# Products of the last MLP blocks as pairs of 64-column halves of the PE array

## The chip, the cores and the metric

The kernel runs on one core of a Trainium2 chip. A core has a matrix engine (PE, with its weight loads listed apart as PEld), a vector engine (DVE), a scalar engine (ACT), a general engine (POOL), a queue engine for transfers (SP), and 16 DMA engines that all queues share. The metric is the device time of one execution in microseconds. The kernel before took 306.42 us as the median of five runs: 306.84, 306.89, 304.28, 306.42 and 304.47 us.

## The reference

A retention layer without softmax is followed by an MLP:

```
q, k, v: 8 batches x 8 heads x 576 positions x 64, float32
scores = (q @ k^T) / 8,  times gamma_h^(i-j) where i >= j, else 0
attn   = scores @ v                       (per batch and head)
x      = attn as 4608 tokens x 512
h      = x @ w_in                         (512 -> 2048)
g      = h * clip(h + 3, 0, 6) / 6
out    = g @ w_out                        (2048 -> 512), float32
```

## The kernel before

**Retention.** Each batch's 576 positions are four chunks of 128 and a tail of 64; two tails share one chunk, so there are 36 chunks. Queries and keys are scaled with powers of gamma while they are cast to fp16, which leaves a plain causal mask for the scores and a running 64x64 state per head for everything before the chunk. `ret1` computes the scores of a chunk: 8 matmuls in 4 pairs (line 283), each with 64 rows of the array (the head dimension) and 128 columns, two heads side by side in the upper and lower half of the rows. DVE multiplies them with the mask (line 294). `ret2` computes the outputs into a PSUM tile `xp`: for each of 4 head pairs, two matmuls of scores times values (line 308) and two of state times queries (line 314, or 321 for tails). Each has all 128 rows and 64 columns of the array; the two of a pair (`z` = 0 and 1) write the PSUM partitions 0 to 63 and 64 to 127. Eight more of that kind (line 333) update the state.

**MLP.** Tokens are taken in nine blocks of 512: blocks 0 to 7 are the first 512 positions of each batch, block 8 holds the eight tails. All blocks together are worked in the order 0, 1, 2, 3, 4, 5, 6, 8, 7. The first product (`up`, line 377) makes 16 groups of 128 hidden units per block, each group 4 matmuls of 128 rows, 128 columns and 512 moving columns. (Blocks 1 and 2, and a few groups of block 0, use `up_half`, line 393, with 256.) ACT and DVE turn each group into a slice of the fp16 tile `g` (lines 360 and 365). The second product is, for all blocks but 0, a scheme of Strassen's kind: 7 products instead of 8 (`product`, line 491), with 16 matmuls of 128 x 128 x 256 each. Four of the seven use sums of quarters of `g` (tiles `ss`), which DVE builds in `enc` (line 455). The products end in the accumulators A, B, C and D; ACT and DVE move them out (lines 497 to 520), and SP stores them. Block 0 uses the plain form (line 420).

**Order.** The order of all work is written out by hand in the string `PROGRAM` (lines 36 to 78), one word per step: `s25` is `ret1` of chunk 25, `o25` its `ret2`, `u5.9` the hidden group 9 of block 5, `e5.1.0.4` a part of `enc`, `P5.0` to `P5.6` the seven products of block 5 in the order P1, P5, P6, P2, P7, P4, P3; `c` are casts, `l` loads, `x` transposes by DMA. Each engine follows its instructions in this order. The steps `s` and `o` of the later chunks are set between the steps `u` and `P` of the earlier blocks. The last retention step, `o35`, stands before `P6.6`; from there to the end PE has only MLP work: block 8, then block 7.

**PE's three shapes.** So PE meets matmuls of three kinds: all rows and columns (`u`, `P`; called wide below), half the rows (`s`), and half the columns (`o`). In the profile's operand lists they are `128*128`, `64*128` and `128*64`.

**PSUM.** The hidden groups and the accumulators share four PSUM buffers (tag `mm`); `xp`, the scores and the state have their own.

Of the kernel before, what the change touches and what calls it, by code (L numbers as in the profile page):

```python
# [83 lines left out]
def kernel(  # L84
# [9 lines left out]
    nc = tc.nc  # L94
    B, H, S, D = q.shape
    NTOK, DM = out.shape
    DFF = moe_w_in.shape[1]
    P = 128
# [4 lines left out]
    NFC = DFF // P  # L103
    NCC = DM // P
    BLK = 512
    gamma = [1.0 - 2.0 ** (-5.0 - h) for h in range(H)]
    lng = [float(np.log(g)) for g in gamma]

# [14 lines left out]
    win16 = const.tile([P, NCC, DFF], FP16)  # L123
    wout16 = const.tile([P, NFC, DM], FP16)
    tmat = [const.tile([P, NFC // 2, 256], FP16, name=f"tmat{i}") for i in range(4)]
    xtail = const.tile([P, NCC, BLK], FP16)
    ident = const.tile([P, P], FP16)
    zero16 = const.tile([P, BLK], FP16)
    NS16 = 2
# [121 lines left out]
    def warm(ps, n, w=P):  # L251
        for _ in range(n):
            nc.tensor.matmul(ps, zero16[:, 0:P], zero16[:, 0:w], start=True, stop=True)
# [46 lines left out]
    def ret2(c):  # L300
# [24 lines left out]
        if kind == 0:  # L325
            if t == 0:
                state[0] = psum.tile([P, HP, D], FP32, tag="st", name="state")
                xts[b] = work.tile([P, NCC, BLK], FP16, tag="xt", bufs=3,
                                   name="xt")
# [25 lines left out]
    def g_new(kb):  # L355
        gs[kb] = work.tile([P, NFC, BLK], FP16, tag="g", bufs=2, name="g")

    def hswish(ph, dst):
        u = work.tile([P, BLK], FP32, tag="u", bufs=3, name="u")
        nc.scalar.activation(u, ph, ACTF.Relu, bias=0.5,  # L360
                             scale=1.0 / 6.0)
        sh = list(dst.shape)
        uv = u if len(sh) == 2 else u.rearrange("p (a i) -> p a i", a=sh[1])
        pv = ph if len(sh) == 2 else ph.rearrange("p (a i) -> p a i", a=sh[1])
        nc.vector.scalar_tensor_tensor(out=dst, in0=uv, scalar=1.0,  # L365
                                       in1=pv, op0=ALU.min, op1=ALU.mult)

    def up(kb, fc, nwarm=0):
        if kb not in gs:
            g_new(kb)  # L370
        g = gs[kb]
        xt = xts[kb] if kb < B else xtail
        ph = psum.tile([P, BLK], FP32, tag="mm", bufs=4, name="ph")
        if nwarm:
            warm(ph[:, 0:P], nwarm)
        for m in range(NCC):
            nc.tensor.matmul(ph, win16[:, m, P * fc:P * fc + P], xt[:, m, :],  # L377
                             start=(m == 0), stop=(m == NCC - 1))
        hswish(ph, g[:, fc, :])

    def up_half(kb, hb, fcs, nwarm=0):

        if kb not in gs:
            g_new(kb)
        g = gs[kb]
        xt = xts[kb]
        ph = psum.tile([P, BLK], FP32, tag="mm", bufs=4, name="ph")
        cs = slice(256 * hb, 256 * hb + 256)
        if nwarm:
            warm(ph[:, 0:P], nwarm)  # L390
        for j, fc in enumerate(fcs):
            for m in range(NCC):
                nc.tensor.matmul(ph[:, 256 * j:256 * j + 256],  # L393
                                 win16[:, m, P * fc:P * fc + P], xt[:, m, cs],
                                 start=(m == 0 and j == 0), stop=(m == NCC - 1),
                                 skip_group_check=True)
        d = fcs[1] - fcs[0]
        hswish(ph, g[:, fcs[0]:fcs[1] + 1:d, cs])

    def store(kb, i0, osb_ap, n0, nn):  # L400

        if kb < B:
            base = kb * S + i0
            nc.sync.dma_start(out[base:base + P, n0:n0 + nn], osb_ap)
        else:
            for z in range(2):
                base = (i0 // TAIL + z) * S + MAIN
                nc.sync.dma_start(out[base:base + TAIL, n0:n0 + nn],
                                  osb_ap[z * TAIL:(z + 1) * TAIL, :])
# [6 lines left out]
    def down_plain_part(kb, pos, f0, f1):  # L416
        g = gs[kb]
        for fc in range(f0, f1):
            for mc, po in enumerate(pos):
                nc.tensor.matmul(po, g[:, fc, P * mc:P * mc + P],  # L420
                                 wout16[:, fc, :],
                                 start=(fc == 0), stop=(fc == NFC - 1))

    def down_plain_end(kb, pos):
        for mc, po in enumerate(pos):
# [8 lines left out]
    HF = NFC // 2  # L434
# [24 lines left out]
    def wq(i, j):  # L459
        return wout16[:, i * HF:(i + 1) * HF, j * 256:(j + 1) * 256]  # L460

    def product(kb, name):
        g = gs[kb]
        d = dn.setdefault(kb, {})

        def gq(i, j):
            return lambda fc, m: g[:, j * HF + fc,
                                   i * 256 + m * P:i * 256 + m * P + P]

        def sq(w):  # L470
            t_ = ssum[(kb, w)]
            return lambda fc, m: t_[:, fc, m * P:m * P + P]

        acc, first, last, lhs, rhs = {
            "P1": ("A", True, False, gq(0, 0), wq(0, 0)),
            "P2": ("A", False, True, gq(0, 1), wq(1, 0)),
            "P6": ("B", True, False, None, tmat[1]),
            "P7": ("B", False, False, None, tmat[2]),
            "P4": ("D", True, True, gq(1, 1), tmat[3]),
            "P5": ("C", True, False, None, tmat[0]),  # L480
            "P3": ("C", False, True, None, wq(1, 1)),
        }[name]
        if lhs is None:
            lhs = sq({"P6": 2, "P7": 3, "P5": 1, "P3": 4}[name])
        if first:
            d[acc] = psum.tile([P, 2, 256], FP32, tag="mm", bufs=4,
                               name="acc" + acc)
        ps = d[acc]
        for fc in range(HF):
            for m in range(2):  # L490
                nc.tensor.matmul(ps[:, m, :], lhs(fc, m), rhs[:, fc, :],  # L491
                                 start=(first and fc == 0 and m == 0),
                                 stop=(fc == HF - 1 and m == 1),
                                 skip_group_check=True)
        if name == "P1":
            d["X"] = work.tile([P, 2, 256], FP32, tag="X", bufs=1, name="X1")
            nc.scalar.copy(d["X"], ps)
        elif name == "P6":
            d["W"] = work.tile([P, 2, 256], FP32, tag="W", bufs=1, name="W1")
            nc.vector.tensor_tensor(out=d["W"], in0=ps, in1=d["X"], op=ALU.add)  # L500
        elif name == "P5":
            return
        else:
            if name == "P7":
                d["Z"] = work.tile([P, 2, 256], FP32, tag="Z", bufs=1, name="Z1")
                nc.vector.tensor_tensor(out=d["Z"], in0=ps, in1=d["X"],
                                        op=ALU.add)
                ps = d["C"]
            ob = work.tile([P, 2, 256], FP32, tag="osb", bufs=4, name="osb")
            if name == "P2":  # L510
                nc.scalar.copy(ob, ps)  # L511
                i, j = 0, 0
            elif name == "P7":
                nc.vector.tensor_tensor(out=ob, in0=ps, in1=d["Z"], op=ALU.add)
                i, j = 1, 1
            elif name == "P4":
                nc.vector.tensor_tensor(out=ob, in0=ps, in1=d["Z"], op=ALU.add)
                i, j = 1, 0
            else:
                nc.vector.tensor_tensor(out=ob, in0=ps, in1=d["W"], op=ALU.add)  # L520
                i, j = 0, 1
            if kb < B:
                base = kb * S + i * 256
                nc.sync.dma_start(
                    out[base:base + 256, j * 256:(j + 1) * 256]
                    .rearrange("(m p) n -> p m n", p=P), ob)
            else:
                for m in range(2):
                    store(kb, i * 256 + m * P, ob[:, m, :], j * 256, 256)
# [87 lines left out]
    for h in range(H):  # L617
        z = h % 2
# [95 lines left out]
```

## Time and profile before

| | |
|---|---|
| median of five runs | 306.42 us |
| the profiled execution | 306.84 us, its span 304.6 us |
| PE busy | 292.7 us (96%), 2879 matmuls |
| weight loads (PEld) busy | 200.9 us (66%) |
| DVE, ACT, POOL busy | 240.1, 145.7, 102.9 us |
| line 377, 128x512 | mean 379 ns from start to end |
| line 491, 128x256 | 273 ns |
| line 308, 128x128 in half the columns | 230 ns |

The durations of matmuls overlap: the next one starts long before the one before has ended. What a matmul costs is the distance between the starts of two that follow each other, and this is read from the timeline. A timeline row gives the start, the length, the engine, the line, the operation and how many instructions were merged into it; the row's length reaches to the end of the last of them. "Idle before" tells how long the engine had nothing to do before a row, and what ended that.

### The profile page before, as it was taken

The page shows a single profiled execution, that of the slowest core. Times are in us where ns is not written, and L with a number is a line of the kernel's source. Part 1 is how long each engine was busy: PE and PEld are TensorE (multiplying, and loading weights), DVE is VectorE, ACT ScalarE, POOL GpSimd, SP SyncE. Part 2 cuts the span into 40 slices and gives each one's busy share as a digit, 9 for nine tenths or more (in the row PEclk, how much of TensorE's full clock was granted, in tenths as well). Part 3 has the DMA queues.
Part 4 walks back from the last instruction along what each step waited for, and adds up shares of the span by engine and source line. Part 5 has one row for each costly group of instructions (what it writes and reads, how often), then busy time and mean ns, then how long its engine had stood idle before and what let it go on. Part 6 is the DMA issues. An engine that isn't in the chain of part 4 may idle for free.

```text
span 304.6 us, 7130 instructions
## 1 busy us (share of the span) xinstructions
PE 292.7 (96%) x2879; PEld 200.9 (66%) x2879; DVE 240.1 (79%) x341; ACT 145.7 (48%) x267; POOL 102.9 (34%) x116
## 2 busy tenths in 40 slices
PE   8789999898999999999999999999999999999995
PEld 3566444687887888646864686468655874684584
DVE  6656845899976999889778996998699768856963
ACT  2578713865236643466147423763376226405610
POOL 5254554884048635445554141334200000000000
PEclk9879999999999999999999999999999999999999
DMA  6999999999999999999999998997603030014003
GB/s 217 303 322 383 253 310 213 225 209 209 196 156 217 229 212 215 195 205 206 237 214 241 242 237 185 225 265 88 178 3 69 28 114 0 1 43 97 2 0 138
DMA packets 149728, 53.93 MB, mean 177 GB/s; under 512 B 134848, under 2 KB 145088, under 8 KB 149696
## 3 DMA queue, kind: packets, MB, share of 16 engines
q1 hardware_dynamic: 120128, 46.15, 69.6%
q10 hardware_dynamic: 29568, 7.34, 17.4%
q8 instruction: 22, 0.36, 0.5%
q14 instruction: 10, 0.08, 0.1%
HBM read 36.70 MB, written 9.44 MB: 151 GB/s over the span
## 4 chain that ended last, share of the span: by engine, by line
PE 88%; DVE 4%; DMA 3%; ACT 2%; issue 0%; SPq 0%
PE ph L377 31%; PE accB L491 10%; PE ph L393 9%; PE accA L491 9%; PE accC L491 9%; PE accD L491 5%; PE po L420 4%; PE xp L308 4%; PE sc L283 4%; DMA g<-in_k_dram 3%; PE xp L314 2%; DVE g L365 2%; PE state L333 1%; DVE ss L455 1%; ACT wout L220 1%; DVE tmat L580 1%
## 5 line engine op out<-in xcount | busy, mean ns | idle before, releaser
L360 ACT ACTIVATE u<-ph 128x512 f32<-128x512 f32 x144 | 84.6, 597 | 65.3 <-PE ph L377 36.8
L365 DVE SCALAR_TENSOR_TENSOR g<-u,ph 128x512 f16<-128x512 f32 x144 | 94.7, 683 | 25.3 <-ACT u L360 24.2
L377 PE MATMUL ph<-xt,win 128*128 128x512 f16 x368 | 82.1, 379 | 0.0
L377 PEld LDWEIGHTS <-win 128*128 128x128 f16 x432 | 41.4, 98 | 47.7
L491 PEld LDWEIGHTS <-ss 128*128 128x128 f16 x512 | 49.0, 98 | 6.9 <-DVE ss L455 0.9
L176 POOL TENSOR_TENSOR qk<-st,tq 128x512 f16<-128x512 f32 x29 | 30.4, 1048 | 51.4 <-DMA st<-in_q_dram 20.9
L176 POOL TENSOR_TENSOR v<-st,tkv 128x512 f16<-128x512 f32 x29 | 32.1, 1111 | 36.5 <-DMA st<-in_v_dram 13.9
L294 DVE TENSOR_TENSOR at<-sc,mask 128x1024 f16<-128x1024 f32 (+1 forms) x34 | 39.0, 1154 | 5.4 <-PE sc L283 5.3
L491 PEld LDWEIGHTS <-g 128*128 128x128 f16 x384 | 36.9, 98 | 6.1 <-issue 0.8
L393 PE MATMUL ph<-xt,win 128*128 128x256 f16 x288 | 34.1, 277 | 0.4 <-ACT xt L338 0.4
L176 POOL TENSOR_TENSOR qk<-st,tkv 128x512 f16<-128x512 f32 x26 | 29.3, 1126 | 10.7 <-PE accA L491 6.7
L491 PE MATMUL accA<-wout,g 128*128 128x256 f16 x256 | 30.6, 273 | 0.8 <-DVE g L365 0.8
L393 PEld LDWEIGHTS <-win 128*128 128x128 f16 x288 | 27.9, 99 | 4.5 <-issue 0.5
L491 PE MATMUL accB<-tmat,ss 128*128 128x256 f16 x256 | 30.7, 273 | 0.1
L338 ACT ACTIVATE xt<-xp 128x512 f16<-128x512 f32 x32 | 19.1, 598 | 20.2 <-PE xp L314 16.9
L455 DVE TENSOR_TENSOR ss<-g 128x1024 f16<-128x1024 f16 (+1 forms) x30 | 23.9, 807 | 0.3
L308 PE MATMUL xp<-at,v 128*64 128x128 f16 x288 | 20.7, 230 | 1.3 <-ACT xt L338 0.8
L308 PEld LDWEIGHTS <-v 128*64 128x64 f16 x288 | 14.8, 112 | 7.3 <-issue 4.8
L511 ACT COPY osb<-accA 128x512 f32<-128x512 f32 x8 | 4.7, 586 | 28.2 <-PE accA L491 28.2
L344 ACT CAST s<-state 64x256 f16<-64x256 f32 x48 | 17.3, 360 | 0.5
L420 PE MATMUL po<-wout,g 128*128 128x512 f16 x64 | 15.0, 379 | 0.6 <-DVE g L365 0.5
L491 PE MATMUL accC<-wout,ss 128*128 128x256 f16 x128 | 15.3, 273 | 0.0
(88 smaller groups left out, 273.8 us busy)
## 6 DMA issues: line engine op xcount, KB each, us to landing
st<-in_v_dram SPq DMA_DIRECT2D x32, 256.0 KB, 6.0
out_dram<-osb SPq DMA_DIRECT2D x32, 256.0 KB, 4.9
st<-in_q_dram SPq DMA_DIRECT2D x28, 256.0 KB, 5.6
st<-in_k_dram SPq DMA_DIRECT2D x28, 256.0 KB, 6.0
wst<-in_moe_w_in_dram SPq DMA_DIRECT2D x4, 512.0 KB, 7.4
tmat<-in_moe_w_in_dram SPq DMA_DIRECT2D x4, 512.0 KB, 8.8
wst<-in_moe_w_out_dram SPq DMA_DIRECT2D x4, 512.0 KB, 10.3
g<-in_moe_w_out_dram SPq DMA_DIRECT2D x4, 512.0 KB, 6.0
```

The costliest lines, as they stand in the source:

```text
L176: eng.tensor_tensor(out=dst, in0=st[:, ix, :, :], in1=tab.unsqueeze(2).to_broadcast([P, H, D]), op=ALU.mult)
L294: nc.vector.tensor_tensor(out=dst, in0=src, op=ALU.mult, in1=m[:, :].unsqueeze(1).to_broadcast([P, n, P]))
L308: nc.tensor.matmul(xp[rows[z], p, :], vt[:, 2 * p + z, :], at[:, z, p, :], start=(p == 0), stop=False, skip_group_check=True)
L338: nc.scalar.activation(xts[b][:, :, t * P:(t + 1) * P], xp, ACTF.Copy, scale=0.125)
L344: nc.scalar.copy(s16[rows[z], :, rows[z]], sp[rows[z], :, :])
L360: nc.scalar.activation(u, ph, ACTF.Relu, bias=0.5, scale=1.0 / 6.0)
L365: nc.vector.scalar_tensor_tensor(out=dst, in0=uv, scalar=1.0, in1=pv, op0=ALU.min, op1=ALU.mult)
L377: nc.tensor.matmul(ph, win16[:, m, P * fc:P * fc + P], xt[:, m, :], start=(m == 0), stop=(m == NCC - 1))
L393: nc.tensor.matmul(ph[:, 256 * j:256 * j + 256], win16[:, m, P * fc:P * fc + P], xt[:, m, cs], start=(m == 0 and j == 0), stop=(m == NCC - 1),
L420: nc.tensor.matmul(po, g[:, fc, P * mc:P * mc + P], wout16[:, fc, :], start=(fc == 0), stop=(fc == NFC - 1))
L455: nc.vector.tensor_tensor(out=dst, in0=a, in1=c, op=op)
L491: nc.tensor.matmul(ps[:, m, :], lhs(fc, m), rhs[:, fc, :], start=(first and fc == 0 and m == 0), stop=(fc == HF - 1 and m == 1), skip_grou ...
```

## The change

Two tuples name the blocks that get the new form. `mul` issues one wide matmul as before, or two in its place. Of the two, the first loads the columns 0 to 63 of the stationary operand and writes the PSUM partitions 0 to 63; the second takes the columns 64 to 127 and the partitions 64 to 127. Both stream the same moving operand. The first product is issued so in blocks 5, 6, 8 and 7, the second in blocks 4, 5, 6, 8 and 7. Everything else, the order in `PROGRAM` included, stays. (Each matmul in the kernel's text becomes a weight load and a matmul on PE.)

```diff
     BLK = 512
+    COL_UP, COL_DOWN = (5, 6, 8, 7), (4, 5, 6, 8, 7)
...
+    def mul(ps, lhs, rhs, start, stop, halves=True):
+
+        if not halves:
+            nc.tensor.matmul(ps, lhs, rhs, start=start, stop=stop,
+                             skip_group_check=True)
+            return
+        for z in range(2):
+            nc.tensor.matmul(ps[z * D:z * D + D], lhs[:, z * D:z * D + D], rhs,
+                             start=start, stop=stop, skip_group_check=True)
+
...
         for m in range(NCC):
-            nc.tensor.matmul(ph, win16[:, m, P * fc:P * fc + P], xt[:, m, :],
-                             start=(m == 0), stop=(m == NCC - 1))
+            mul(ph, win16[:, m, P * fc:P * fc + P], xt[:, m, :],
+                m == 0, m == NCC - 1, kb in COL_UP)
         hswish(ph, g[:, fc, :])
...
             for mc, po in enumerate(pos):
-                nc.tensor.matmul(po, g[:, fc, P * mc:P * mc + P],
-                                 wout16[:, fc, :],
-                                 start=(fc == 0), stop=(fc == NFC - 1))
+                mul(po, g[:, fc, P * mc:P * mc + P], wout16[:, fc, :],
+                    fc == 0, fc == NFC - 1, kb in COL_DOWN)
...
         for fc in range(HF):
             for m in range(2):
-                nc.tensor.matmul(ps[:, m, :], lhs(fc, m), rhs[:, fc, :],
-                                 start=(first and fc == 0 and m == 0),
-                                 stop=(fc == HF - 1 and m == 1),
-                                 skip_group_check=True)
+                mul(ps[:, m, :], lhs(fc, m), rhs[:, fc, :],
+                    first and fc == 0 and m == 0, fc == HF - 1 and m == 1,
+                    kb in COL_DOWN)
```

`up_half` is changed in the same way; it is used by blocks 0 to 2 alone, which are in neither tuple.

More of the change, by code (lines that the diff above doesn't have):

```diff
@@ L392, in up_half @@
             for m in range(NCC):
-                nc.tensor.matmul(ph[:, 256 * j:256 * j + 256],
-                                 win16[:, m, P * fc:P * fc + P], xt[:, m, cs],
-                                 start=(m == 0 and j == 0), stop=(m == NCC - 1),
-                                 skip_group_check=True)
+                mul(ph[:, 256 * j:256 * j + 256],
+                    win16[:, m, P * fc:P * fc + P], xt[:, m, cs],
+                    m == 0 and j == 0, m == NCC - 1, kb in COL_UP)
         d = fcs[1] - fcs[0]
@@ L490, in product @@
             for m in range(2):
-                nc.tensor.matmul(ps[:, m, :], lhs(fc, m), rhs[:, fc, :],
-                                 start=(first and fc == 0 and m == 0),
-                                 stop=(fc == HF - 1 and m == 1),
-                                 skip_group_check=True)
+                mul(ps[:, m, :], lhs(fc, m), rhs[:, fc, :],
+                    first and fc == 0 and m == 0, fc == HF - 1 and m == 1,
+                    kb in COL_DOWN)
         if name == "P1":
```

## The prediction

> **What bounds the kernel now.** I began with the page's busy rows, to see which engine is full, and where.
>
> ```profile
> PE 292.7 (96%) x2879; PEld 200.9 (66%) x2879; DVE 240.1 (79%) x341; ACT 145.7 (48%) x267; POOL 102.9 (34%) x116
> PE   8789999898999999999999999999999999999995
> DVE  6656845899976999889778996998699768856963
> PEclk9879999999999999999999999999999999999999
> ```
>
> PE is full from about the tenth slice on, at full clock. That alone doesn't say that PE sets the pace, since a busy PE can still be running below its rate. So the second view is the table by stretches, cut where the change bites: the first product in the new form is P4.0, which I place at 171.6 us (the accA rows of the trace; block 4's first product is the seventh of them), and the last retention step ends at 246.7.
>
> ```profile
> core 0: us, PE busy (x) PEld busy (x) DVE busy (x) ACT busy (x) POOL busy (x), PEclk, DMA share, GB/s
> 171.60:247.00 75.40, 75.40 (x817) 52.76 (x812) 66.50 (x90) 33.66 (x65) 16.43 (x15) 1.00 0.72 142
> 247.00:301.00 54.00, 53.88 (x368) 35.50 (x365) 38.31 (x55) 21.88 (x37) 0.00 (x0) 1.00 0.16 46
> 301.00:304.60 3.60, 0.00 (x0) 0.00 (x0) 0.61 (x1) 0.00 (x0) 0.00 (x0) 0.81 0.37 127
> ```
>
> For 129 us PE is never idle but for 0.12 us; after it come one DVE addition and the last store, 3.6 us. The list of waits of PE in this stretch is empty. So what shortens PE's own sequence there shortens the kernel, if nothing else then becomes late. The third view, the timeline of PE, shows at what rate it works and where it loses time:
>
> ```profile
> 201.94 1.91 PE L491 MATMUL accA<-wout,g 128*128 128x256 f16 x16
> 203.69 1.91 PE L491 MATMUL accC<-tmat,ss 128*128 128x256 f16 x16
> 205.53 0.40 PE L283 MATMUL sc<-qkT 64*128 64x128 f16 x8
> 205.86 0.25 PE L308 MATMUL xp<-at,v 128*64 128x128 f16 x2
> 205.94 0.22 PE L314 MATMUL xp<-qkT,s 128*64 128x128 f16 x2
> ...
> 206.33 0.29 PE L333 MATMUL state<-v,qk 128*64 128x64 f16 x8
> 206.55 1.92 PE L491 MATMUL accB<-tmat,ss 128*128 128x256 f16 x16
> 208.31 1.91 PE L491 MATMUL accA<-wout,g 128*128 128x256 f16 x16
> 210.15 0.25 PE L308 MATMUL xp<-at,v 128*64 128x128 f16 x2
> 210.23 0.22 PE L314 MATMUL xp<-qkT,s 128*64 128x128 f16 x2
> ```
>
> *Rate of wide matmuls.* From 201.94 to 203.69 are 16 of them: 109 ns each. In the chain, 40 of line 377 take 8.63 us, 216 ns each. The two give 0.416 ns a moving column and 2.6 ns besides.
>
> *Rate of pairs.* From 205.94 to 206.33 are seven column pairs of 128: 55.7 ns a pair. The line above gives 128 x 0.416 + 2.6 = 55.8. So the two halves run at once, and a pair costs what one wide matmul of that length would. Starts of single instructions show the second half 3 to 4 ns behind the first, and the next pair 52 to 53 ns later.
>
> *Changes of shape.* The last accC matmul starts at 203.69 + 1.91 - 0.273 = 205.33; the scores follow at 205.53, 0.20 us later where 0.109 is the rate. In the same way every change of shape shows a gap. From single starts, which repeat within 2 ns from 130 us to 247, the excess at the change and at the next step is:
>
> ```
> wide -> half rows     96 + 10 = 106 ns
> half rows -> columns  90 + 24 = 114
> columns -> wide       99 + 10 = 109
> wide -> columns       94 + 24 = 118
> columns -> half rows  99 + 11 = 110
> half rows -> wide     92 + 11 = 103
> ```
>
> Nothing else exceeds the rate in this stretch, but two waits of some 65 ns for an `ss` tile, at 265.9 and 292.0.
>
> **The change part by part.**
>
> *Changes of shape removed.* Going through PROGRAM from P4.0 on, 25 boundaries are touched. Columns to wide, now without any change: o23 P4.0, o24 P4.3, o25 P4.6, o26 u5.2, o27 u5.6, o28 P5.2, o31 u6.3, o32 u6.12, o33 P6.0, o34 P6.4, o35 P6.6: 11 x 109 ns = 1.20 us. Wide to columns, likewise: P5.3 o29, u6.1 o30, P6.5 o35: 3 x 118 = 0.35 us. Still a change, but of another kind: before s25 to s29 and s32 to s35 (9 times) columns instead of wide to half rows, 9 x 4 = 0.04 us dearer; after s30 and s31 half rows to columns instead of wide, 114 instead of 103 at most, 0.02 us dearer. Block 4's first product stays wide, so nothing changes before P4.0. Saved: 1.55 - 0.06 = **1.5 us**, all of it on PE and before 246.7.
>
> *Pairs for wide matmuls.* First product: 4 blocks x 16 x 4 = 256 pairs of 512. Second: 5 x 7 x 16 = 560 pairs of 256. 816 pairs in all, so PE shows 2879 + 816 = 3695 matmuls. No row shows a pair of 256 or 512. The nearest is the pair of 128, and it lies on the line of the wide ones, so I take 0 ns a pair. Bounds: above, the 3.3 ns between the halves might come on top of each pair, 816 x 3.3 = +2.7 us; below, the 2.6 ns that every start costs might vanish, -2.1 us, but the pair of 128 pays it too, so a gain has no row for it.
>
> *Weight loads.* [...] The rows:
>
> ```profile
> L491 PEld LDWEIGHTS <-ss 128*128 128x128 f16 x512 | 49.0, 98 | 6.9 <-DVE ss L455 0.9
> L308 PEld LDWEIGHTS <-v 128*64 128x64 f16 x288 | 14.8, 112 | 7.3 <-issue 4.8 <-DVE osb L514 0.2
> ```
>
> A half's load takes 112 ns where a whole one takes 98. If the two loads of a pair went one after the other, a pair of 256 would take 224 ns instead of 109, and the 560 of them 64 us more. But in retention four instructions (two such loads, two matmuls) fit into each 56 ns, and the state's pairs of 64 columns come every 30 ns; the loads of the two halves run side by side and behind the matmuls before. A pair of 256 leaves them 109 ns. [...]
>
> [...]
>
> *Instruction supply.* PE gets 1632 instructions more. The page's queue 8 fetched 22 packets of 0.36 MB in all, 16 KB each; one took 0.9 to 1.4 us, about one for every 256 of PE's instructions. After the change some 28. In the new products 256 instructions last 7 us; the trace before has 261 in 7 us at 114 us, with DMA at its fullest and no gap on PE beyond the changes of shape. Cost 0; if each of the some 15 fetches after 171 us stood open, 15 x 1.2 = 18 us.
>
> *Who is late next.* ACT and DVE get no work and no wait. A PE that is 1.5 us ahead by 247 asks them to be quicker by as much over 75 us, of which DVE is busy 66.5. In its tightest 20 us (190 to 210: 19.34 busy) three changes go, 0.33 us of PE's time, against 0.66 idle. Single margins: a PSUM buffer for a hidden group comes free 0.4 us (u6.14) to 2 us before PE wants it; the `ss` tile of P5.2 and that of P6.2 are there 0.6 us before, and one change of shape (0.11) goes between the last `u` and them; transposed chunks land 2.7 us or more before their scores. None is used up. What lies behind 247 us, the two 65 ns waits included, moves forward as a whole.
>
> *Sum.* 306.84 - 1.5 = 305.3 us for an execution like the profiled one. That one lies 0.4 us above the median, so 306.42 - 1.5 = **304.9 us**, 0.5% less. The runs shown lie at 304.3 to 304.5 and 306.4 to 306.9, with nothing between, so a median can fall 2 us to either side without the kernel being another. About 1% is what a measurement of this kernel can tell from no change.
>
> **The rivals.**
>
> *The pair is dearer than one wide matmul (slower).* Place: every pair, the 129 us after 171.6. The change loses from 1.5 us / 816 = 1.8 ns a pair, and loses over 1% from 5.6 ns. With the offset between the halves on top, 304.9 + 2.7 = 307.6; with the slower load on the path (14 ns), 304.9 + 11.4 = 316.3. For it: no row at 256 or 512, two streams of one operand instead of one for long times, and the load's row. Against it: the 55.7 ns. Chance 0.13, 0.06 of it at the small price.
>
> *Instructions come too late.* 304.9 + 18 = 323. For it: the rate is above the one shown over spans longer than 7 us (448 in 12.2 us; before at most 431 in 14 us). Against it: fetches are short beside 7 us. Chance 0.03.
>
> *The gain is waited off.* DVE, 97% busy from 190 to 210, holds PE back, and the time stays at 306.4. For it: u6.14's 0.4 us. Against it: DVE's own gaps there end with ACT, which waited for PE. Chance 0.11.
>
> *The change does more than counted*, by over 1%: 303 or less. No row for it; 0.04.
>
> **How the numbers follow.** The forecast keeps 0.69. About an eighth of it falls below 303.4, by the spread of the runs. Faster by over 1%: 0.09 + 0.04 = 0.13. Slower by over 1%: 0.07 + 0.03 = 0.10. Within 1%: 0.77. The range goes from 302.7 (the forecast with a median 2 us low) to 307.6 (the small price of a pair); it leaves out the dear cases above and a few per cent below.
>
> **What the profile would show.** Right: rows of line 491 and 377 with `128*64`, pairs of 256 every 109 ns and of 512 every 216; no gap between `o` and `u` or `P` from 171.6 on; P6.0 about 1.2 us earlier than 234.4, the first group of block 8 starting at about 247.0 instead of 248.5; 52.4 us from there to the end of PE, as before; 3695 matmuls. Wrong: over 111 ns a pair, gaps every 256 instructions, or waits of PE for DVE between 190 and 247.

## The result, and the profile after

The changed kernel takes 305.35 us (median; 302.69 to 307.48), the kernel before 305.88 us in the same comparison. The ratio is 0.9972, with a 95% interval of 0.9956 to 0.9988: 0.28% faster, or 0.86 us, with 0.37 to 1.35 us in the interval. The plain medians lie 0.53 us apart, the means 0.80 (standard error 0.24). Forecast was 1.5 us. So the direction and the range held, and 0.6 us of the gain is missing. That the median comes within 0.5 us of the forecast's 304.9 is in part luck: the forecast started from 306.42, the median of five runs, and over more runs the kernel before lies 0.54 lower. The profiled execution took 305.91 us, its span is 303.7.

First the page of the kernel after: busy rows, the queue that fetches instructions, and the weight loads of the halves from `ss`.

```profile
PE 289.3 (95%) x3695; PEld 208.9 (69%) x3695; DVE 238.8 (79%) x341; ACT 145.2 (48%) x267; POOL 103.5 (34%) x116
...
q8 instruction: 29, 0.48, 0.7%
...
L366 PEld LDWEIGHTS <-ss 128*64 128x64 f16 x640 | 34.5, 110 | 0.5 <-DVE ss L464 0.3
```

The matmuls are 3695, as counted. The instruction queue fetched 29 packets (before 22; 28 were forecast). A half's weight load takes 110 ns on average, where a whole one took 98, so the slower load is really there. PE's busy time fell all the same, by 3.4 us, but that also holds differences of the first 125 us, where executions of one kernel differ (two of before by 2.7 us).

The table by stretches shows whether PE is still the bound; the cuts are moved to this execution.

```profile
core 0: us, PE busy (x) PEld busy (x) DVE busy (x) ACT busy (x) POOL busy (x), PEclk, DMA share, GB/s
171.20:245.50 74.30, 74.30 (x1275) 58.09 (x1276) 66.39 (x91) 33.73 (x65) 15.36 (x15) 1.00 0.84 145
245.50:300.10 54.60, 54.47 (x760) 40.73 (x754) 39.02 (x56) 22.07 (x37) 0.00 (x0) 1.00 0.16 46
```

PE is busy throughout at full clock, and weight loads rose to 58.09 us beside it without showing as a gap. PE's list of waits is empty from 165 us on. The timeline of PE has the same steps as the one shown of before:

```profile
201.94 1.91 PE L366 MATMUL accA<-wout,g 128*64 128x256 f16 x32
203.69 1.91 PE L366 MATMUL accC<-tmat,ss 128*64 128x256 f16 x32
205.54 0.40 PE L284 MATMUL sc<-qkT 64*128 64x128 f16 x8
...
206.34 0.29 PE L334 MATMUL state<-v,qk 128*64 128x64 f16 x8
206.46 1.92 PE L366 MATMUL accB<-tmat,ss 128*64 128x256 f16 x32
208.21 1.91 PE L366 MATMUL accA<-wout,g 128*64 128x256 f16 x32
209.96 0.22 PE L309 MATMUL xp<-at,v 128*64 128x128 f16 x2
```

Three things are read here. A product of 32 halves takes 1.75 us from start to start (201.94 to 203.69), as 16 wide ones did: a pair costs 109 ns. From the state's first matmul to accB's is 0.12 us (206.34 to 206.46), where it was 0.22: the change from columns to wide is gone. From accA to the next outputs is 1.75 us, where it was 1.84: wide to columns is gone as well. The scores still cost a change on both sides: from accC to them are 1.85 us and from them to the outputs 0.32, where it was 1.84 and 0.33.

To leave out what lies ahead of the change, I measure from the first scores of chunk 24 to the end of PE's last matmul. First before, then after:

```profile
170.69 0.40 PE L283 MATMUL sc<-qkT 64*128 64x128 f16 x8
...
298.97 1.91 PE L491 MATMUL accC<-wout,ss 128*128 128x256 f16 x16
```

```profile
171.21 0.40 PE L284 MATMUL sc<-qkT 64*128 64x128 f16 x8
...
298.06 1.91 PE L366 MATMUL accC<-wout,ss 128*64 128x256 f16 x32
```

PE ends at 300.88 and 299.97. That is 130.19 us before and 128.76 after: **1.43 us less**, against 1.5 forecast. So the two profiles show nearly the full gain, and the comparison of all runs 0.86 us. The experiments ask what each term of the sum is worth, and where the rest stays.

### The profile page after: what moved, and what is told of

Its sections match the earlier page's. It is cut to its first block, busy times and chain, and to the rows that moved or that the text cites. A ratio compares the mean times of both kernels' runs of the same rounds, so it can differ in the third digit from the quotient of the medians.

```text
span 303.7 us, 8762 instructions
## 1 busy us (share of the span) xinstructions
PE 289.3 (95%) x3695; PEld 208.9 (69%) x3695; DVE 238.8 (79%) x341; ACT 145.2 (48%) x267; POOL 103.5 (34%) x116
## 4 chain that ended last, share of the span: by engine, by line
PE 82%; SPq 5%; DVE 5%; DMA 3%; ACT 1%; POOL 1%; issue 1%; ACTq 0%; POOLq 0%
PE ph L366 18%; PE ph L362 17%; PE accB L366 6%; PE accC L366 6%; PE accA L366 6%; PE po L362 4%; SPq L555 4%; PE accB L362 4%; PE xp L309 3%; DMA tmat<-in_moe_w_in_dram 3%; PE sc L284 3%; PE accA L362 3%; PE accC L362 3%; PE accD L366 3%; DVE g L376 2%; PE accD L362 2%
## 5 line engine op out<-in xcount | busy, mean ns | idle before, releaser
L362 PE MATMUL ph<-xt,win 128*128 128x256 f16 (+1 forms) x464 | 72.6, 313 | 1.9 <-ACT xt L339 1.3
L362 PEld LDWEIGHTS <-win 128*128 128x128 f16 x464 | 44.4, 98 | 25.3 <-issue 2.5
L366 PEld LDWEIGHTS <-win 128*64 128x64 f16 x512 | 28.7, 110 | 24.4
L366 PE MATMUL ph<-xt,win 128*64 128x512 f16 x384 | 42.8, 379 | 0.0
L366 PEld LDWEIGHTS <-ss 128*64 128x64 f16 x640 | 34.5, 110 | 0.5 <-DVE ss L464 0.3
L362 PEld LDWEIGHTS <-g 128*128 128x128 f16 x208 | 19.6, 98 | 11.3 <-issue 2.8
L366 PEld LDWEIGHTS <-g 128*64 128x64 f16 x480 | 26.1, 110 | 0.6
L362 PEld LDWEIGHTS <-ss 128*128 128x128 f16 x192 | 18.4, 98 | 2.7 <-DVE ss L464 0.4
L366 PE MATMUL accB<-tmat,ss 128*64 128x256 f16 x320 | 19.2, 273 | 0.0
L366 PE MATMUL accA<-wout,g 128*64 128x256 f16 x320 | 19.1, 273 | 0.0
```

Source lines behind the costliest of these rows:

```text
L362: nc.tensor.matmul(ps, lhs, rhs, start=start, stop=stop, skip_group_check=True)
L366: nc.tensor.matmul(ps[z * D:z * D + D], lhs[:, z * D:z * D + D], rhs, start=start, stop=stop, skip_group_check=True)
```

## The experiments

Theory 1 is the prediction's: pairs are free, only changes of shape count, and nothing else becomes late. The rivals are dearer pairs, late instructions, and a gain that is waited off.

**Before and after, again.** Neither is edited.

> The kernel before, unchanged, against itself: it shows how far a comparison of this length lies from 1 by chance. Every theory says 306 us and a ratio of 1.000; a ratio beyond 0.998 to 1.002 would mean that the 0.28% measured for the change is within what chance gives.

> The change as it is. Theory 1 (14 changes of shape fewer, pairs cost nothing, all of it comes through): from the scores of chunk 24 to the end of PE 129.4 us where the kernel before takes 130.9, and a ratio of 0.995. Theory 2 (the gain in that stretch is real, but the stretch before it gets slower by some 0.5 us, by instruction supply or placement): the same 129.4, but the scores of chunk 24 start 0.5 us later than in the kernel before, ratio 0.997. Theory 3 (a part of the gain is waited off in some executions): more than 129.8 us in that stretch.

Before gave 306.05 us, ratio 0.9992 (0.9966 to 1.0018). After gave 305.33, ratio 0.9979 (0.9952 to 1.0006), so this comparison alone can't tell it from before. In the new profiles the stretch from chunk 24's scores to PE's end is 130.20 us and 128.76 us. The stretch thus repeats within 0.01 us, and the change is worth 1.44 us in it. (The totals in the expectation, 130.9 and 129.4, are 0.7 us too large on both sides; the difference is what counts.) In these profiles all that varies lies ahead: chunk 24's scores start at 170.69 and 167.99 us in the two profiles of before, at 171.21 and 169.15 in the two of after. In both pairs the change comes later here, by 0.52 and 1.16 us, as the second theory of the expectation has it. But three more profiles, of the next three kernels below, have the code of before up to this place and start at 168.53, 168.71 and 169.21. With a scatter of nearly 3 us from one code, a loss of some 0.5 us ahead of the change can be neither shown nor excluded.

**Pairs in blocks 8 and 7 alone.** Behind the last retention step there is no shape to be matched, so this gives the price of the pair alone.

```diff
-    COL_UP, COL_DOWN = (5, 6, 8, 7), (4, 5, 6, 8, 7)
+    COL_UP, COL_DOWN = (8, 7), (8, 7)
```

> Pairs in blocks 8 and 7 alone: 128 pairs of 512 and 224 of 256, with no retention beside them, so no change of shape goes and one comes (before the first group of block 8). Theory 'a pair costs one wide matmul': from the first group of block 8 to the last product the same 52.4 us within 0.1, the whole +0.1 us. Theory 'the offset between the halves adds up': 352 x 3.3 ns = +1.2 us. Theory 'the slower load is on the path': 352 x 14 ns = +4.9 us.

306.39 us, ratio 1.0001 (0.9972 to 1.003). In the chain of before, `P6.6` and the last product start at

```profile
246.79 1.85 PE accC L491 x16
...
299.13 1.76 PE accC L491 x16
```

which is 52.34 us apart; in the chain of this kernel

```profile
244.64 1.85 PE accC L362 x16
...
297.14 1.77 PE accC L366 x32
```

they lie 52.50 apart. One change, wide to columns, is new between the two (118 ns by the prediction's list; from block 8's own first start to PE's end, as the expectation counts, it is 52.47 us against 52.40); 0.04 us is left for 352 pairs, 0.1 ns a pair. "The pair is dearer" would need 1.8 ns a pair to undo the gain. That rival falls.

**Quarters.** Four parts of 32 columns double the instructions once more, and with them any offset between the parts (3 to 4 ns between halves).

```diff
-        for z in range(2):
-            nc.tensor.matmul(ps[z * D:z * D + D], lhs[:, z * D:z * D + D], rhs,
-                             start=start, stop=stop, skip_group_check=True)
+        for z in range(4):
+            nc.tensor.matmul(ps[z * 32:z * 32 + 32], lhs[:, z * 32:z * 32 + 32],
+                             rhs, start=start, stop=stop, skip_group_check=True)
```

The tuples are again `(8, 7), (8, 7)`.

> Blocks 8 and 7 alone, each wide matmul as four of 32 columns in place of two of 64: PE gets 2112 instructions more than before, 8 in each 109 ns of the second products, 256 of them in 3.5 us. Theory 'only the moving columns count': 52.1 us from the first group of block 8 to the last product, as before, and a time within 0.2 us of before. Theory 'each further part adds its 3 ns': 352 x 9 ns = +3.2 us in that stretch. Theory 'instructions come too late': gaps on PE some every 3.5 us. Beside this: if a longer PE program by itself makes the first 125 us slower (the change came out some 0.7 us short of what its late stretch gained, for 1632 instructions more), the whole is about 0.9 us slower than the stretch explains; if not, the two agree.

306.21 us, ratio 1.0013 (0.9989 to 1.0037). The chain:

```profile
244.82 1.85 PE accC L362 x16
...
286.74 1.75 PE accA L366 x64
...
297.32 1.78 PE accC L366 x64
```

Again 52.50 us, and 64 quarters take 1.75 us, as 32 halves and 16 wholes do. Eight instructions (four loads, four matmuls) every 109 ns leave no gap. "Instructions come too late" falls, and so does an offset that adds up by the part. The expectation asked one thing more: whether a longer PE program slows the first 125 us by itself, which would show as some 0.9 us beyond the stretch. This kernel is 0.4 us slower than before (-0.3 to 1.1 by its interval), and the stretch explains 0.16 us of it; so no such loss shows, but the interval doesn't exclude it.

**Shapes in turn.** In blocks 8 and 7 the hidden groups 0 to 7 are pairs and 8 to 15 wide; `PROGRAM` takes one of each in turn.

```diff
-    COL_UP, COL_DOWN = (5, 6, 8, 7), (4, 5, 6, 8, 7)
+    COL_UP, COL_DOWN = (8, 7), ()
...
-                m == 0, m == NCC - 1, kb in COL_UP)
+                m == 0, m == NCC - 1, kb in COL_UP and fc < 8)
```

> First products of blocks 8 and 7 alone: groups 0 to 7 in halves, groups 8 to 15 wide, second products wide. The order takes them in turn (0, 8, 1, 9, ...), so 16 changes of shape are added per block, 32 in all, and 64 matmuls become pairs. Price of a change as read in the prediction (109 ns columns to wide; 94 ns and up to 24 for wide to columns): 32 x 0.103 to 0.114 = +3.3 to +3.6 us, ratio 1.011 to 1.012. Theory 'a change of shape costs little by itself and the gaps before were those of retention's waits': under +1 us.

309.97 us, ratio 1.0126 (1.0087 to 1.0166). The timeline shows the price at each group:

```profile
247.10 1.05 PE L366 MATMUL ph<-xtail,win 128*64 128x512 f16 x8
248.09 1.04 PE L362 MATMUL ph<-xtail,win 128*128 128x512 f16 x4
249.06 1.05 PE L366 MATMUL ph<-xtail,win 128*64 128x512 f16 x8
```

Groups start 0.97 to 0.99 us apart where 4 x 0.216 = 0.864 is the rate. The chain:

```profile
245.32 1.85 PE accC L362 x16
...
301.29 1.76 PE accC L362 x16
```

`P6.6` and the last product are 55.97 us apart, 3.63 more than before. That is 32 changes at 113 ns; the prediction's 109 and 118 in equal parts would be 113.5.

**All blocks.** If shapes are all that counts, pairs in every block should gain more.

```diff
-    COL_UP, COL_DOWN = (5, 6, 8, 7), (4, 5, 6, 8, 7)
+    COL_UP, COL_DOWN = tuple(range(9)), tuple(range(9))
```

> Pairs in all nine blocks: 75 changes of shape in place of 110 before and 96 with the change. By the prices of the prediction 3.7 us of PE's time less than before, 2.2 less than with the change. Theory 1: what lies after 125 us (0.6 us more than with the change) comes through whole; what lies before it only where PE doesn't wait for loads there; so 302.5 to 304.3, ratio 0.988 to 0.994. Theory 'instructions come too late where the DMA engines are full' : gaps on PE in the first 170 us and no gain, or a loss, over the change.

316.5 us, ratio 1.0301 (1.0259 to 1.0344): a clear miss. (The built program has 79 changes of shape, not the 75 of the expectation.) From chunk 24's scores on it takes 128.76 us, as with the change; the whole loss lies ahead of them. The waits of PE between 90 and 170 us, as engine, line, what it waited for, sum in us, how often, the longest; first before:

```profile
PE xp L308 <- DVE at L294: 0.5, 1, 0.5
PE ph L393 <- ACT xt L338: 0.4, 1, 0.4
```

then with pairs in all blocks:

```profile
PE ph L366 <- DVE g L376: 6.7, 3, 5.2
PE sc L284 <- DMA qkT<-qk: 1.8, 2, 0.9
...
```

PE waits for DVE to finish a hidden group, once for 5.2 us. So something holds back the evacuation of the groups. Two more kernels look for it, one that widens the change by a single block, and one that puts pairs where they hurt and nowhere else.

```diff
-    COL_UP, COL_DOWN = (5, 6, 8, 7), (4, 5, 6, 8, 7)
+    COL_UP, COL_DOWN = (3, 4, 5, 6, 8, 7), (3, 4, 5, 6, 8, 7)
```

> Pairs in block 3 and in the first product of block 4 too: six changes of shape fewer than with the change (90 against 96), 0.6 us of PE's time, all after 122 us. Theory 'PE is the bound from 125 us on and the feed has room': 129.2 us from the scores of chunk 24 to the end of PE as with the change or less, from the first group of block 3 to those scores 44.8 instead of 45.3 us, ratio 0.993 to 0.995. Theory 'the feed of chunks by loads and transposes has no room before 170 us' (what the run with all blocks suggests): waits of PE for scores or for PSUM between 125 and 170 us, and no gain over the change.

```diff
-    COL_UP, COL_DOWN = (5, 6, 8, 7), (4, 5, 6, 8, 7)
+    COL_UP, COL_DOWN = (0, 1, 2), (0, 1, 2)
```

> Pairs in blocks 0 to 2 alone: 13 changes of shape fewer, 1.4 us of PE's time, all before 125 us, where PE also waits for loads. Theory 'PE gets ahead of the feed there, ACT then stands behind transposes whose data aren't loaded, and PSUM isn't freed': PE waits for g of 1 us and more between 105 and 145 us and a time of 309 us or more, as with all blocks. Theory 'the loss with all blocks came from block 3': the time is 306 or less.

From block 3 on: 309.43 us, ratio 1.0084 (1.0057 to 1.0112). Six changes of shape fewer than after, and yet slower; PE waits, but nearly all of it just before 193 us, and only 0.25 us between 125 and 170, where one side had expected it. From chunk 24's scores on its profile takes 133.07 us, 4.31 more than with the change; the medians differ by 4.1. Blocks 0 to 2: 317.82, ratio 1.0388 (1.0348 to 1.0428). The timeline of the first of the two, some rows around the wait (SPq and ACTq are the transfers' issues on SP and ACT):

```profile
184.88 1.60 SPq L162 DMA_DIRECT2D st<-in_v_dram  x2
...
185.77 0.60 ACT L371 ACTIVATE u<-ph 128x512 f32<-128x512 f32 x1 [0.27 <-PE ph L366]
...
190.11 1.28 ACTq L185 DMA_TRANSPOSE qkT<-qk  x1
...
191.50 1.08 ACT L371 ACTIVATE u<-ph 128x512 f32<-128x512 f32 x2 [5.12 <-POOL v L177]
...
192.12 1.28 DVE L376 SCALAR_TENSOR_TENSOR g<-u,ph 128x512 f16<-128x512 f32 x2 [5.04 <-ACT u L371]
...
192.87 0.41 PE L366 MATMUL ph<-xt,win 128*64 128x512 f16 x2 [2.88 <-DVE g L376]
```

ACT stands idle for 5.12 us behind one instruction, the transpose of chunk 28's queries and keys (a step `x`), though two finished groups (`u5.1` and `u5.9`) lie in PSUM. When it goes, ACT, DVE and PE follow within 3 us. The releaser named, a cast on POOL, belongs to chunk 30 (`c30` stands behind `o26` in `PROGRAM`) and gives chunk 28 nothing. What the transpose waited for is seen in the landings: the value load issued at 184.88 us landed at 190.01, and the transpose was issued at 190.11.

The kernel's text is built into lists of instructions for each engine, with their waits; these built programs tell why a transpose should wait for a load. DMAs issued by SP and ACT share eight completion semaphores: in the traces of before and after 208 transfers, 26 on each. The builder hands these out in turn, as it seems in the order in which it places the transfers (the first 40 issued take them in turn), and in the programs each transfer waits until the one before it on its semaphore has landed. In these two traces none is issued earlier; the shortest distance is 0.02 us. In the kernel from block 3 on, the load of 184.88 us and the transpose of 190.11 us have the same one. Chunk 28's transpose, in the built program of before and of after:

```
before: qkT_3104<-qk16_2856  waits DMAHW3_49, DMAHW5_49, DVE_49, Pool_49
after:  qkT_3224<-qk16_2856  waits DMAHW3_49, DMAHW7_49, DVE_49, Pool_49
```

(The number in a semaphore's name, `DMAHW5` or `DMAHW7`, tells which of the eight it is.) The instructions of ACT, DVE, POOL and SP are the same ones, but a transpose shares its semaphore with another load, and that can be one issued later (chunk 29's follows a load issued 5.2 us ahead of it in after, 8.1 us in before). In the kernel with pairs in blocks 0 to 2, the transpose that ends the long wait went at 137.20 us, 0.06 us after the landing (137.14) of a key load issued at 131.42 on the same semaphore. Six transposes in a row (chunks 15 to 20) went 0.06 to 0.10 us after the landing of the transfer before them on their semaphore: three loads, two stores and one transpose. In before these six distances are 2 to 9 us. (Before is not free of such waits: there chunk 22's transpose goes 0.10 us after chunk 21's has landed.) Against before, the transposes' waits differ from chunk 8 on in this kernel and in the one with all blocks, from chunk 22 on with block 3, from chunk 28 on in the change itself, and nowhere in the three kernels that alter blocks 8 and 7 alone. Why pairs move the builder's order was not shown.

A second cost shows in the same kernel (pairs in blocks 0 to 2): PE's row after its wait, and the table cut at the wait. The table's columns are those above, the clock third from the end.

```profile
140.31 5.62 PE L362 MATMUL ph<-xt,win 128*128 128x512 f16 x16 [5.09 <-DVE g L376]
```

```profile
136.00:140.30 4.30, 0.00 (x0) 0.00 (x0) 0.73 (x2) 1.36 (x3) 1.32 (x2) 0.68 1.22 282
140.30:144.30 4.00, 3.99 (x10) 1.43 (x10) 3.04 (x5) 1.69 (x4) 0.00 (x0) 0.50 1.35 194
144.30:148.00 3.70, 3.70 (x46) 1.89 (x44) 3.29 (x5) 2.05 (x5) 1.24 (x2) 0.99 1.38 218
```

After the wait of 5 us PE runs at a clock of 0.50 for some 4 us: ten matmuls in 4.0 us, 427 ns apart instead of 216. That adds some 1.9 us to the 5 us. All of PE's waits between 90 and 170 us sum to 10.1 us in this kernel (0.9 in before); with the 1.9 us this is most of the loss of 12 us.

**Is it a faster PE instead?** It might be that PE merely runs ahead of ACT and DVE. So pairs stay in blocks 0 to 2, but the first and the last matmul of each stretch of MLP work between two retention steps are wide. The changes of shape come back and more: the built program has 152, before has 110.

```diff
+    edge = [False, 0, 0]
...
-        if not halves:
+        edge[1] += 1
+        if not halves or edge[1] == 1 or (edge[0] and edge[1] == edge[2]):
```

(A dozen lines in the loop over `PROGRAM` set `edge`; the tuples are `(0, 1, 2)`.)

> Pairs in blocks 0 to 2 as in the run that lost 12 us, but the first and the last matmul of every stretch of MLP work between two retention steps stay wide. So no change of shape goes and about two come per stretch: PE has some 3.5 us more to do before 125 us than in the kernel before, and isn't ahead of its input. Theory 'the loss comes from waits that the built program got: a transpose shares its completion semaphore with a load issued shortly before, and ACT stands until that load has landed': those waits are nearly the same as in the run that lost, so 314 us or more, with PE waiting over 4 us for g at about 140 us. Theory 'PE got ahead of its input by the changes saved': 306 to 310 us, no such wait.

314.22 us, ratio 1.0254 (1.0208 to 1.0301). PE's waits between 90 and 170 us:

```profile
PE xp L309 <- ACT xt L339: 1.8, 1, 1.8
PE sc L284 <- DMA qkT<-qk: 1.3, 1, 1.3
PE ph L364 <- DVE g L378: 1.3, 1, 1.3
...
```

PE now has more to do than in before, 42 changes or some 4.6 us, which is about half of the loss of 8.4 us. And it still waits, if less: 4.6 us in this stretch, where it was 10.1 with pairs throughout and 0.9 in before. Six transposes (chunks 15 to 20) again go 0.06 to 0.15 us after the landing of the transfer before them on their semaphore. So a PE that runs ahead by the changes saved isn't the cause. The long wait at 140 us, which I had expected to stay above 4 us, did not stay: the longest in this stretch is 1.8 us. And some of this kernel's waits differ from those of the kernel it was made from (five of its 28 transposes have another semaphore), so it doesn't isolate one wait.

**Transposes on SP.** If ACT no longer issues them, a late transpose can't hold up ACT.

```diff
-        nc.scalar.dma_start_transpose(
+        nc.sync.dma_start_transpose(
```

> All matmuls wide as before, but the 28 transposes of the chunks are issued by SP, in the place that they have among the loads in the written order, and not by ACT. All transfers then stand on one queue, and which two share a semaphore no longer hangs on anything but that order. It is the partner of the run with pairs in all blocks and the same issue by SP. Level unknown: SP waits for casts before it can issue later loads; 304 to 325 us.

> Pairs in all nine blocks, transposes issued by SP. Waits of SP, ACT and, but for four, of POOL and DVE are those of its partner with wide matmuls. Theory 'shared semaphores made the loss of 10 us with all blocks, the pairs themselves cost nothing also with the DMA engines full': faster than the partner by 1 to 3.7 us (35 changes of shape fewer). Theory 'pairs in the first blocks run PE ahead of its input or are short of instructions': slower than the partner by several us, as it was on ACT's queue.

Before with this edit takes 320.44 us, ratio 1.046 (1.0422 to 1.0498); all blocks in pairs with it 322.33, ratio 1.052 (1.0478 to 1.0563). The expected gain of pairs in the second over the first didn't come: it is 0.6% slower (four runs of each). PE's waits between 60 and 200 us, in the first and in the second:

```profile
PE sc L283 <- DMA qkT<-qk: 12.5, 4, 5.8
...
```

```profile
PE sc L284 <- DMA qkT<-qk: 15.7, 4, 6.8
...
```

On SP the transposes stand among the loads, and PE waits for transposed chunks in both, for 12.5 and 15.7 us. The edit brings a larger wait of its own, and the pair of runs says nothing for or against the semaphores.

**Pairs only where no wait changes.** Pairs are set by place instead of block: only in the stretches of MLP work between two retention steps from `u5.2` on. In this form every wait of ACT, SP, POOL and DVE in the built program is that of before, and 11 changes of shape go.

```diff
-    COL_UP, COL_DOWN = (5, 6, 8, 7), (4, 5, 6, 8, 7)
+    PAIRED, gap = (26, 27, 28, 29, 30, 31, 32, 33, 34, 35), [-1, False]
...
-                m == 0, m == NCC - 1, kb in COL_UP)
+                m == 0, m == NCC - 1, gap[1])
...
+    after_ret = True
     for w in PROGRAM.split():
+        if w[0] in "soS":
+            after_ret = True
+        elif w[0] in "uhP" and after_ret:
+            after_ret = False
+            gap[0] += 1
+            gap[1] = gap[0] in PAIRED
```

(The other calls of `mul` get `gap[1]` in the same way.)

> The change cut to the stretches of MLP work after the scores of chunk 27 (from u5.2 on): 11 changes of shape fewer than before in place of 14, and every wait of ACT, SP, POOL and DVE as in the kernel before. Theory 'the change gains 1.45 us on PE and gives about 0.7 back by the new waits of the transposes of chunks 28 and 29 in some executions': 1.2 us from the scores of chunk 24 to the end of PE (129.7 instead of 130.9), all of it in the median: ratio 0.996, not slower than with the change, and the transposes of chunks 28 and 29 start 1.9 us and more after the load whose semaphore they share has landed (0.1 with the change). Theory 'the shortfall of the median comes from the first 125 us': ratio 0.998.

305.54 us, ratio 0.9962 (0.9933 to 0.9991). The stretch from chunk 24's scores on is 129.07 us, 1.12 less than before, where 11 changes were to give 1.2. The transposes of chunks 28 and 29 go 4.15 and 5.66 us after the landing on their semaphore, as expected. The means of its 14 runs and of before's differ by 1.11 us (standard error 0.42), which is the gain of the stretch; for the change itself they differ by 0.80 (0.24) where the stretch gives 1.43. This would fit a loss through the moved waits. But the difference between 1.11 and 0.80 is less than one standard error, and the medians, in which the whole gain was expected, are only 0.32 us apart (305.86 and 305.54), less than the 0.53 us of the change. So this run doesn't decide.

## Why the prediction was right, and where it was not

*What bounds the kernel.* Right: what was taken from PE's own sequence after 170 us came out of the stretch, and PE waited for nothing there in the profiles of the change. From the first hidden group of block 3 to chunk 24's scores, before and after take 46.37 us alike (124.31 to 170.69, and 124.83 to 171.21), so the change touches nothing there. What it does in the first 124 us is open: the profiles scatter too much.

*Changes of shape removed.* Right in size: 1.43 and 1.44 us of 1.5 in two pairs of profiles, and 113 ns a change in the kernel with shapes in turn. `P6.0` comes 62.59 us after chunk 24's scores instead of 63.73 (1.14 earlier; 1.2 forecast), block 8's first group 76.32 instead of 77.79 (1.47; 1.5 forecast). From there to PE's end it is 52.44 us, before 52.40.

*Pairs, weight loads, instruction supply.* All three were costed at nothing, and all three are right: 0.1 ns a pair by one kernel, and quarters as quick as halves by another (1.75 us a product). A half's load is slower in the row (110 ns against 98), and it costs no time here: a product of 32 halves takes the 1.75 us of 16 wholes. (The rival's 11.4 us are the 14 ns between its rows of 112 and 98 ns, for each of the 816 pairs; nothing of it came.)

*Who is late next.* This step failed: "ACT and DVE get no work and no wait". They get no work, but some of their waits change. In the change as it stands, 19 instructions of SP, ACT, POOL and DVE carry other waits, on ACT from the transpose of chunk 28 on. In its profiled execution the wait costs nothing on PE, but it is visible; ACT's rows before and after:

```profile
188.16 1.29 ACTq L184 DMA_TRANSPOSE qkT<-qk  x1
189.56 1.08 ACT L360 ACTIVATE u<-ph 128x512 f32<-128x512 f32 x2 [0.94 <-DMA st<-in_v_dram]
```

```profile
188.73 1.25 ACTq L185 DMA_TRANSPOSE qkT<-qk  x1
190.08 1.09 ACT L371 ACTIVATE u<-ph 128x512 f32<-128x512 f32 x2 [1.24 <-DMA st<-in_v_dram]
```

In before, chunk 28's transpose went 1.9 to 2.5 us after the load on its semaphore had landed; in both profiles of after it went 0.10 us after, which is to say that it waited for it. (On ACT this is little: idle for 1.24 and 1.11 us instead of 0.94, and most of that is the issue itself.) A load that lands later in some execution would hold ACT there, as it did for 5 us in the kernel from block 3 on; no trace of the change shows that. PE never waited for it in the two profiles of after.

*The size.* Of 1.5 us, 0.86 (0.37 to 1.35) arrived. Three accounts are left. The term mis-sized is the one above, taken as nothing, if the moved waits take the rest in some executions; the means of the kernel without them fit this, its medians do not. Or the change loses some 0.5 us in the first 124 us; its two profiles hint at this, within a scatter of nearly 3 us. Or it is chance: the interval ends at 1.35 us, just short of the 1.43 of the stretch, and that of the repeated comparison reaches from a loss of 0.2 us to a gain of 1.5. Only profiled executions can be looked into, and those show the full gain. So the cause of the missing 0.6 us is not settled. What is shown is that waits move and what this costs at its worst: 5 us waits, and 3.9% where pairs stand in blocks 0 to 2. A kernel with pairs in all blocks and the waits of before was not tried.

*The rivals.* "The pair is dearer" and "instructions come too late" are excluded by runs. "The gain is waited off" named DVE between 190 and 210 us; DVE didn't hold PE up there. Of its kind another turned up, in the semaphores, and it decides against the wider versions of this change. No version beats the change beyond doubt: the one with unmoved waits and the change can't be told apart.

## What to carry to other kernels

Read the price of a change of array shape from the starts of single instructions; where it is a tenth of a microsecond (103 to 118 ns here) and neighbours alternate, giving the neighbours one shape is worth the number of changes times that price on the engine itself (14 changes fewer, 1.43 us here); splitting a wide matmul into halves that share a moving operand cost nothing on the full PE here (0.1 ns a pair). After any edit that alters the number of instructions, though it be on one engine alone, compare the waits of all engines in the built programs before and after: a transfer can inherit another predecessor on its semaphore, as chunk 28's transpose did (`DMAHW7` for `DMAHW5`). With pairs from block 3 on, ACT stood idle for 5.12 us behind that one transpose, so a transfer issued from an engine with other work deserves the first look.

## What was not expected of the hardware

After PE had stood still for 5.1 us (pairs in blocks 0 to 2), its clock was 0.50 for about 4 us, and 512-column matmuls came 427 ns apart instead of 216; that wait cost some 1.9 us more than itself. After one of 2.88 us (pairs from block 3 on) the clock stayed at 1.00. And four quarter matmuls with their four loads, eight instructions in 109 ns, ran as fast as one whole matmul and its load (64 quarters and 16 wholes in 1.75 us each).
